# A fused attention and mixture-of-experts kernel: first chunk ahead of the loop, rows of x earlier in it, the branch moved up, pools that wait by tile

## The chip, the core and the metric

One program on one core of a Trainium2 chip. The metric is the time of one execution on the device in microseconds (us); lower is better. Five engines run their own instruction streams in order: TensorE (PE; its weight loads are listed as PEld), VectorE (DVE), ScalarE (ACT), GpSimd (POOL) and SyncE (SP, which issues most DMA transfers). They wait for each other through semaphores.

## What is computed

Three parts follow each other: a gated linear attention over 4 x 8 heads of 768 steps, a layer of eight experts in which each takes at most 384 of 3072 tokens (tokens choose in the order of their logits), and a dense ELU layer.

```python
# attention, per batch and head; f = sigmoid(f_logit)
for t in range(S):
    state = f[t, :, None] * state + outer(k[t], v[t])
    y[t] = q[t] @ state
x = y as 3072 rows of 384
# experts
logits = x @ w_gate
for idx in argsort(-logits.flatten()):
    tok, e = idx // E, idx % E
    if assigned[tok] >= 0 or counts[e] >= cap: continue
    assigned[tok] = e; counts[e] += 1
out[assigned == e] = relu(x[assigned == e] @ w1[e]) @ w2[e]
# dense layer
h = out @ w_in
return where(h > 0, h, exp(min(h, 0)) - 1) @ w_out
```

## The kernel before

**Attention.** The 3072 rows are cut into NJ = 24 chunks of 128 (six for each batch). All heads of a chunk go together, in four pairs. The order of the work is written by hand: one pass `j` of a loop from -5 to 23 holds steps of several chunks, and each engine runs its own share in that order. For a chunk: `load` (f, v, k and q by SyncE), `decayE` and `decayL` (an exponential and a logarithm on ScalarE, of two chunks at once; for the first two chunks one at a time), `decays` (L473, TensorE sums the logarithms with a triangular mask), `prepW` and `prepP` (L477, L481, exponentials of the sums on ScalarE), `prepK` and `prepQ` (L486, L490, k and q times these on VectorE), `scores` (L502, TensorE), `masked` (L523, VectorE), `turn` and `turned` (L509, L516: the keys turned on TensorE, copied out on ScalarE), `state`, `carry`, `carried` (L535 to L543), `ystep` (L554, L560), `yout` (L565), `xrows` (L574: TensorE turns y into rows of x and the logits of the gate), `xout` (L578), `xstore`, `lout` (L584). In a pass TensorE runs state(j), scores(j+1), turn(j+1), ystep(j), xrows(j-1), decays(j+3). The last chunk of each six has no turn and no state.

**Weights of the dense layer** ride along: `Conv` loads a block of 512 columns of 64-bit numbers per pass, unpacks it on VectorE (`bits`, L287 to L294), rounds it on ScalarE (`hi`, L301) and takes the difference on GpSimd (`lo`, L308), since a product is made of a high and a low half of each operand.

**Counting.** `best` finds each token's best expert, `reach` (L607) compares its logit with a grid of 256 thresholds, `counted` (L614) sums over tokens on TensorE. From the sums L760 to L769 find the threshold `least` above which no expert is over its 384.

**Ids.** `slots` gives each token above the threshold its place: sums on TensorE, a scan and sums on VectorE, then one-hot rows `oh` (L828 on ScalarE, L834 on VectorE) whose products with `R0` give the first 256 ids of the first expert (`pm0`, L840, read at L843) and with `Rm` all ids (`pm`, L849, read at L850). `gather0` (L857) fetches the first 256 rows of x, `gatherL` (L864) the logits of tokens without a place. `during` runs `feed` in between: it loads weights of an expert (`raw`, L213, six buffers), rounds them on ScalarE (`pc_h`, L229) and takes the low half on VectorE (`pc_l`, L222). Then all engines load `fi`, which says whether a general routine has to do the attention and the choice again, and branch at L871 (with these inputs the routine is skipped).

**Experts.** `xtrans` (L1095) transposes gathered rows, `F1` (L1113) multiplies with a block of w1, `F2` (L1100 to L1102) with a block of w2; eight of each make an expert. `tick` puts the steps of the late choice (L899 to L973: tokens without a place, round by round) between them. The dense layer (L1215 and on) follows each expert.

`spin` issues matmuls on a scratch tile whose result nobody reads.

**Pools.** Tiles come from pools that open and close. A pool opened on bytes of closed pools makes its tiles wait for every user of those.

## Time and profile before

| | us |
|---|---|
| median of 3 runs | 833.48 |
| runs | 838.24, 830.11, 833.48 |
| profiled execution, device time | 838.72 |
| its span, first to last instruction | 837.0 |
| TensorE busy, share of the span | 800.5, 96% |
| VectorE busy | 478.9, 57% |
| ScalarE busy | 414.8, 50% |
| GpSimd busy | 109.0, 13% |
| mean granted TensorE clock | 0.978 |

How the views are read. A row of the timeline or of the chain that ended last begins with its start and its length in us; then engine, line, operation, what is written and read, the shape, and a count where several were merged (their length is then that of the stretch). In brackets stands how long the engine was idle before it, and what ended that. A row of a table by stretch gives the stretch, its length, the busy time of each engine with its instructions, the granted TensorE clock (1.00 is 2.4 GHz, 0.50 is 1.2 GHz), the share of the DMA engines and their GB/s. Instructions on TensorE overlap; a matmul's row includes its way through the array.

### The profile page before, as it was taken

Reading aid. Unit: us, or ns where it says so; the run is one execution under the profiler, and the core shown is the slowest. Engines: PE = TensorE matmul, PEld = TensorE weight load, DVE = VectorE, ACT = ScalarE, POOL = GpSimd, SP = SyncE. Lnnn points to the kernel's source line nnn. Section 1 sums busy time; section 2 is a strip of 40 time slices with the busy share of each in tenths; the row PEclk is TensorE's granted clock in tenths of the full one; section 3 lists DMA queues with packets and bytes.
Section 4 is the critical chain, followed back from the end, with each engine's and each line's share of the span. In section 5 each row is a group of like instructions: output and inputs, shape, how many; then the busy total and the mean of one; then the engine's idle time right before and its main releaser. Section 6 shows DMA issues by size and latency. Waiting matters only on the chain.

```text
span 837.0 us, 15862 instructions
## 1 busy us (share of the span) xinstructions
PE 800.5 (96%) x6123; PEld 755.1 (90%) x6123; DVE 478.9 (57%) x1199; ACT 414.8 (50%) x883; POOL 109.0 (13%) x157
## 2 busy tenths in 40 slices
PE   7899999858989999999999999999999999999996
PEld 6788887658889999999999989999999999999996
DVE  5998888736676755675564345533354335434432
ACT  6566665313554544454445445544445445543442
POOL 2222222220242000300100031000120020001001
PEclk9999999868999999999999998999999999999999
DMA  9998986322043300420041036200051023002000
GB/s 267 261 290 266 287 247 177 89 56 63 1 135 101 98 10 1 138 70 1 13 140 38 1 105 189 76 20 0 20 162 38 1 85 95 29 1 67 1 1 28
DMA packets 41668, 76.75 MB, mean 92 GB/s; under 512 B 8816, under 2 KB 30576, under 8 KB 41584
## 3 DMA queue, kind: packets, MB, share of 16 engines
q1 hardware_dynamic: 38384, 66.20, 26.5%
q0 software_dynamic: 3200, 9.46, 3.5%
q8 instruction: 49, 0.80, 0.4%
q14 instruction: 35, 0.29, 0.1%
HBM read 66.09 MB, written 9.55 MB: 90 GB/s over the span
## 4 chain that ended last, share of the span: by engine, by line
PE 64%; issue 9%; DVE 4%; ACT 1%; POOL 1%; POOLq 0%; DVEq 0%; ACTq 0%
PE ha L1215 20%; PE ha L1113 12%; PE yo L1100 10%; PE yo L1102 10%; PE yo L1101 10%; PE ha L1095 1%; DVE pc_l L222 1%; POOL out L1279 1%; DVE oh L938 1%; DVE elu L1219 0%; PE rt L948 0%; DVE oh L940 0%; ACT h_h L1117 0%; DVE oh L941 0%; PE rt L928 0%
## 5 line engine op out<-in xcount | busy, mean ns | idle before, releaser
L1219 DVE SCALAR_TENSOR_TENSOR elu<-elu,ha 128x384 f32<-128x384 f32 (+2 forms) x128 | 70.8, 554 | 157.2 <-ACT elu L1218 157.2
L1215 PE MATMUL ha<-yt_h,wi_h 128*128 128x384 f32 (+2 forms) x384 | 130.7, 340 | 0.3 <-DVE elu L1219 0.3
L1215 PE MATMUL ha<-yt_h,wi_l 128*128 128x384 f32 (+2 forms) x384 | 129.6, 338 | 0.0
L1100 PE MATMUL yo<-wo_h,g_h 128*128 128x384 f32 x381 | 129.4, 340 | 0.0
L1102 PE MATMUL yo<-wo_h,g_l 128*128 128x384 f32 x381 | 128.5, 337 | 0.0
L1101 PE MATMUL yo<-wo_l,g_h 128*128 128x384 f32 x381 | 128.1, 336 | 0.0
L1215 PE MATMUL ha<-yt_l,wi_h 128*128 128x384 f32 (+2 forms) x384 | 126.1, 335 | 0.0
L1217 ACT ACTIVATE elu<-ha 128x384 f32<-128x384 f32 (+2 forms) x128 | 62.8, 491 | 115.7 <-PE ha L1215 114.1
L1082 ACT ACTIVATE g_h<-elu 128x384 fp32r<-128x384 f32 (+2 forms) x127 | 66.4, 523 | 70.0 <-DVE elu L1219 69.8
L1083 DVE TENSOR_TENSOR g_l<-elu,g_h 128x384 fp32r<-128x384 f32 (+2 forms) x112 | 64.5, 576 | 48.9 <-ACT g_h L1082 47.5
L1117 ACT ACTIVATE h_h<-ha 128x384 fp32r<-128x384 f32 (+2 forms) x72 | 32.7, 455 | 114.7 <-PE ha L1113 104.0
L1118 DVE SCALAR_TENSOR_TENSOR h_l<-ha,h_h 128x384 fp32r<-128x384 f32 (+2 forms) x72 | 36.9, 512 | 83.2 <-ACT h_h L1117 80.0
L1279 POOL DMA_INDIRECT out<-ot,permL x22 | 22.7, 1031 | 432.3 <-ACT ot L1277 428.9
L1113 PE MATMUL ha<-xt_h,pc_l 128*128 128x384 f32 (+2 forms) x216 | 72.0, 334 | 4.0 <-DVE pc_l L222 4.0
L222 DVE TENSOR_TENSOR pc_l<-raw,pc_h 128x384 fp32r<-128x384 f32 x144 | 74.6, 555 | 0.6 <-ACT pc_h L229 0.5
L1215 PEld LDWEIGHTS ha<-yt_h,wi_l 128*128 128x128 f32 x384 | 72.1, 188 | 2.2
L1215 PEld LDWEIGHTS ha<-yt_h,wi_h 128*128 128x128 f32 x384 | 72.2, 188 | 2.0 <-DVE elu L1219 0.5
L1215 PEld LDWEIGHTS ha<-yt_l,wi_h 128*128 128x128 f32 x384 | 71.9, 188 | 1.5
L1113 PE MATMUL ha<-xt_h,pc_h 128*128 128x384 f32 (+2 forms) x216 | 71.9, 333 | 0.6 <-ACT xt_h L1082 0.6
L1100 PEld LDWEIGHTS yo<-wo_h,g_h 128*128 128x128 f32 x381 | 71.6, 188 | 0.9 <-ACT g_h L1082 0.3
L1101 PEld LDWEIGHTS yo<-wo_l,g_h 128*128 128x128 f32 x381 | 71.6, 188 | 0.6
L1102 PEld LDWEIGHTS yo<-wo_h,g_l 128*128 128x128 f32 x381 | 71.6, 188 | 0.3 <-DVE g_l L1083 0.3
(253 smaller groups left out, 1523.3 us busy)
## 6 DMA issues: line engine op xcount, KB each, us to landing
raw<-w SPq DMA_DIRECT2D x144, 192.0 KB, 2.4
ld_kq<-kq SPq DMA_DIRECT2D x24, 448.0 KB, 9.7
r<-win SPq DMA_DIRECT2D x12, 512.0 KB, 5.5
r<-wout SPq DMA_DIRECT2D x12, 512.0 KB, 4.6
vt<-vP SPq DMA_DIRECT2D x12, 384.0 KB, 7.5
x_d<-x SPq DMA_DIRECT2D x24, 192.0 KB, 2.6
ld_f<-fP SPq DMA_DIRECT2D x11, 384.0 KB, 6.3
ld_f<-fP SPq DMA_DIRECT2D x2, 192.0 KB, 3.8
```

The lines of the kernel that those rows point to most:

```text
L222: nc.vector.tensor_tensor(l, RAW.pop(i), h.bitcast(F32), op=OP.subtract)
L1082: nc.scalar.activation(hi, src, AF.Copy)
L1083: (eng or nc.vector).tensor_tensor(lo, src, hi.bitcast(F32), op=OP.subtract)
L1100: nc.tensor.matmul(o, wh, mh, start=start, stop=False)
L1101: nc.tensor.matmul(o, wh, ml, start=False, stop=False)
L1102: nc.tensor.matmul(o, wl, mh, start=False, stop=stop)
L1113: nc.tensor.matmul(p[:, :n], a[:, d * 128:(d + 1) * 128], b[:, d, :n], start=i == 0, stop=i == 8)
L1117: nc.scalar.activation(h[:, :n], p[:, :n], AF.Relu)
L1118: nc.vector.scalar_tensor_tensor(l[:, :n], p[:, :n], 0.0, h[:, :n].bitcast(F32), op0=OP.max, op1=OP.subtract)
L1215: nc.tensor.matmul(p, a[:, d * 2048 + f * 128:d * 2048 + (f + 1) * 128], b[:, d, :N], start=i == 0, stop=i == 8)
L1217: nc.scalar.activation(e, p, AF.Relu, scale=-1.0)
L1219: nc.vector.scalar_tensor_tensor(e, e, -1.0, p, op0=OP.add, op1=OP.max)
```

## The change

The first chunk is issued ahead of the loop, which now begins at pass 0. In a pass TensorE runs state(j), turn(j+1), xrows(j-1), scores(j+1), ystep(j), decays(j+3); `xout`, `xstore` and `lout` move up by one chunk, and `hi` of the dense weights follows `xout`. k and q have three tiles of their own, and the third load is issued ahead of the loads of the gate weights. Some memsets and copies at the start change places; `spin` reads one constant tile. The checks `okp` to `badp` come after the last `reach`. In `slots` six weight blocks are rounded in two groups of three, and five low halves are taken on GpSimd (`lows`): two ahead of `gather0`, three behind it. The branch follows these; `Rm`, the product for all ids and `gatherL` come behind it, the product between the two parts (six and three matmuls) of the first two `F1`. The pools behind the attention let each tile wait only for the users of its own bytes.

```diff
-SPIN = (9, 24, 3, 7, 12)
-WARM = 22
+SPIN = (9, 24, 3, 10, 8, 4, 12)
+WARM = 14
+WARM2 = 4
...
+    def lows(n, eng):
+        for _ in range(n):
+            i = nxt["lo"]
+            h, l = PC[order[i]]
+            eng.tensor_tensor(l, RAW.pop(i), h.bitcast(F32), op=OP.subtract)
+            nxt["lo"] += 1
...
-            KQ[j] = ld.tile([112, 2, 4, 128], F32, name="ld_kq", bufs=3)
-            nc.sync.dma_start(KQ[j].rearrange("p n r t -> p (n r t)"), kq[j])
...
+    KQs = [att.tile([112, 2, 4, 128], F32, name=f"kq{i}") for i in range(3)]
+    KQ = {j: KQs[j % 3] for j in range(NJ)}
...
     load(0, "v")
-    for t in VT:
-        nc.gpsimd.memset(t[:, 768:], 0.0)
+    load(2, "kq")
+    nc.vector.memset(onesB, 1.0)
+    usum = att.tile([128, NJ], F32, name="usum")
+    nc.vector.memset(usum, 0.0)
...
-    spin(ps.tile([128, 1024], F32, name="sc"), WARM)
+    pre = ps.tile([128, 1024], F32, name="sc")
+    spin(pre, WARM)
     one, two = slice(0, 1), slice(1, 2)
-    for j in range(-5, NJ):
-
-        if j >= 3:
-            xstore(j - 3)
...
+    decayE(0, one)
+    decayL(0, one)
+    decays(0)
+    spin(pre, WARM2)
+    prepW(0)
+    prepP(0)
+    decayE(0, two)
+    decayL(0, two)
+    prepK(0)
+    prepQ(0)
+    turn(0)
+    scores(0)
+    decays(1)
+    turned(0)
+    masked(0)
+    decayE(2)
+    prepW(1)
+    prepP(1)
+    decayL(2)
+    prepK(1)
+    prepQ(1)
+    state(0)
+    ystep(0)
+    decays(2)
+    load(4, "f")
+    load(6, "f")
+    conv.load()
+    yout(0)
+    for j in range(NJ):
+
+        if j >= 2:
+            xstore(j - 2)
...
+        prepW(j + 2)
+        prepP(j + 2)
+
+        if j:
+            state(j)
+        turn(j + 1)
+        if j >= 1:
+            xrows(j - 1)
+        scores(j + 1)
+        turned(j + 1)
+        if j >= 1:
+            xout(j - 1)
         if j >= 1:
             conv.hi()
-        if j >= 2:
-            xout(j - 2)
...
-        if j >= 0:
-            state(j)
-        if j + 1 >= 0:
-            scores(j + 1)
-            turn(j + 1)
-            turned(j + 1)
...
-        if j >= 1:
-            xrows(j - 1)
-        if j + 3 >= 0:
-            decays(j + 3)
+        decays(j + 3)
...
-    g0 = ctx.enter_context(tc.tile_pool(name="g0", bufs=1))
+    g0 = ctx.enter_context(tc.tile_pool(name="g0", bufs=1, reuse_waits="tile"))
...
+        if ahead:
+            feed(3, False)
         R0 = tiles(3 * EARLY[0], 2, G)
...
+        if ahead:
+            feed(GAP_FEED - 3, False)
...
         V.tensor_scalar(fi, f1, 0.0, None, op0=OP.is_lt)
+        if ahead:
+            lows(2, G)
...
         V.tensor_scalar(perm0, pm0, 1536.0, None, op0=OP.add)
         gather0()
-        Rm = tiles(0, 28, V)
-        during()
-        spin(wm, SPIN[4])
-        for k in range(NJ):
-            nc.tensor.matmul(pm, oh[:, k, :], Rm[:, k, :], start=k == 0, stop=k == NJ - 1)
-        V.tensor_scalar(permE, pm, 1536.0, None, op0=OP.add)
-        V.tensor_copy(permF, pm)
+        if ahead:
+            lows(GAP_LOW - 2, G)
...
-    slots(lambda: feed(GAP_LOW + 1))
-    feed(GAP_FEED - GAP_LOW - 1, False)
-    gatherL()
+    slots(True)
     rv = nc.values_load(fi[0:1, 0:1], min_val=0, max_val=1, skip_runtime_bounds_check_because="a comparison gives 0 or 1")
     with tc.If(rv > 0):
...
-        gatherL()
+    Rm = tiles(0, 28, nc.vector)
...
+    spin(fh.tile([128, 512], F32, name="ha", bufs=3), SPIN[3])
+    xtrans(0)
+    spin(fh.tile([128, 512], F32, name="ha", bufs=3), SPIN[4])
+    F1a(0, 0)
+    F1a(0, 1)
+    pm = mt["tt"].rearrange("p a e c -> p (a e c)")[:, :28]
+    for k in range(NJ):
+        nc.tensor.matmul(pm, mt["oh"][:, k, :], Rm[:, k, :], start=k == 0, stop=k == NJ - 1)
+    F1b(0, 0)
+    F1b(0, 1)
+    nc.vector.tensor_scalar(permE, pm, 1536.0, None, op0=OP.add)
+    nc.vector.tensor_copy(permF, pm)
+    gatherL()
```

## Rows read from the trace of the kernel before

**Rows 1.** Busy time by stretch: the 100 us from 500 on

```profile
500.00:600.00 100.00, 98.90 (x517) 92.48 (x518) 45.19 (x81) 49.87 (x98) 2.95 (x4) 0.97 0.22 66
```

**Rows 2.** Who waited for whom, 40 to 140 us: engine, line, releaser; sum, times, longest

```profile
DVE am L523 <- PE sc L502: 12.6, 17, 1.4
```

**Rows 3.** Timeline of TensorE's weight loads, one pass of the loop

```profile
104.40 0.85 PEld L554 LDWEIGHTS y<-am,vt 128*64 128x64 f32 x16
...
106.01 0.97 PEld L574 LDWEIGHTS lp<-IW,yt 112*128 112x128 f32 x8 [0.18 <-issue]
107.08 0.83 PEld L473 LDWEIGHTS L<-mask,u 128*48 128x48 f32 x16
107.89 0.60 PEld L535 LDWEIGHTS kv<-vt,kn 128*64 128x64 f32 x16
```

**Rows 4.** Timeline of the opening, ScalarE

```profile
5.80 0.52 ACT L459 ACTIVATE u<-ld_f 128x384 f32<-128x384 f32 x1 [3.69 <-DVE usum L440]
```

**Rows 5.** Timeline of VectorE, chunks 2 and 3

```profile
18.06 0.95 DVE L486 TENSOR_TENSOR kk<-ld_kq,W 112x512 f32<-112x512 f32 x1 [0.54 <-DMA ld_kq<-kq]
...
24.33 1.21 DVE L523 TENSOR_TENSOR am<-sc,mask 128x1024 f32<-128x1024 f32 x1
...
25.73 0.68 DVE L486 TENSOR_TENSOR kk<-ld_kq,W 112x512 f32<-112x512 f32 x1
```

**Rows 6.** DMA, 0 to 40 us: GB/s in each of 40 slices

```profile
GB/s 0 12 270 345 303 393 315 284 256 304 132 285 358 360 238 283 250 331 401 280 222 282 242 262 229 292 265 271 388 289 256 367 253 256 156 127 132 163 131 323
```

**Rows 7.** Busy time by stretch, cut where the granted clock changes

```profile
148.50:151.90 3.40, 3.40 (x35) 2.70 (x35) 3.07 (x16) 0.74 (x2) 1.59 (x1) 0.50 0.24 64
...
172.40:192.90 20.50, 16.02 (x69) 14.19 (x69) 6.84 (x26) 5.10 (x12) 1.96 (x3) 0.50 0.15 42
```

**Rows 8.** Timeline behind the loop: first ids, and TensorE behind the branch

```profile
165.91 0.16 DVE L843 TENSOR_SCALAR permA<-pm 128x2 int32<-128x2 f32 x1 [0.30 <-PE pm L840]
...
173.27 1.65 PE L628 MATMUL ha<-triU,onesB 128*128 128x256 bf16 x7 [4.73 <-PEq L871]
```

**Rows 9.** Timeline at the loop's end: VectorE's last compares, GpSimd's subtraction

```profile
151.28 0.28 DVE L607 TENSOR_SCALAR ge<-grid,top 128x256 bf16<-128x256 bf16 x1
...
154.87 1.56 DVE L607 TENSOR_SCALAR ge<-grid,top 128x256 bf16<-128x256 bf16 x2
...
155.09 1.26 POOL L308 TENSOR_TENSOR wo_l<-w,wo_h 128x512 fp32r<-128x512 f32 x1 [4.97 <-ACT wo_h L301]
```

**Rows 10.** Timeline of the ids: VectorE's builds, GpSimd's multiply

```profile
162.59 2.77 DVE L834 TENSOR_TENSOR oh<-iota,lo 128x768 f16<-128x768 f16 x3
...
162.81 0.87 POOL L820 TENSOR_TENSOR Rm<-Rm,idc 128x48 f16<-128x48 f16 x1 [1.02 <-DMA raw<-w]
```

**Rows 11.** Chain that ended last, from the transposes to the second F1

```profile
174.92 1.33 PE ha L1095 x6
...
176.82 4.22 PE ha L1113 x18
...
181.48 0.42 DVE h_l L1118
```

**Rows 12.** Groups, 160 to 176 us: busy, mean ns | idle before, releaser

```profile
L864 POOL DMA_INDIRECT LU<-lg_d,permA x4 | 3.8, 953 | 1.2 <-issue 1.2
L857 POOL DMA_INDIRECT xg<-x_d,permA x2 | 2.8, 1410 | 3.0 <-DVE permA L843 2.7 <-issue 0.3
...
L849 PE MATMUL tt<-Rm,oh 128*128 128x28 f16 x24 | 0.8, 175 | 0.6 <-DVE Rm L820 0.6
```

**Rows 13.** Timeline of the first expert: a low half, the choice, a low half

```profile
186.76 0.58 PE L1102 MATMUL yo<-h_h,pc_l 128*128 128x256 f32 x1 [2.04 <-DVE pc_l L222]
...
191.34 0.18 DVE L917 TENSOR_TENSOR w<-LU,pen 128x32 f32<-128x32 f32 x1
...
193.39 0.39 PE L1113 MATMUL ha<-xt_h,pc_l 128*128 128x256 f32 x1 [0.50 <-DVE pc_l L222]
```

**Rows 14.** The page's DMA issues: weights of an expert

```profile
raw<-w SPq DMA_DIRECT2D x144, 192.0 KB, 2.4
```

More of the change, by code (lines that the diff above doesn't have):

```diff
@@ L372 @@
                             pattern=[[1, 128]], channel_multiplier=-1)
+    nc.gpsimd.memset(idn, 0.0)
+    nc.gpsimd.affine_select(out=idn, in_=idn, compare_op=OP.not_equal, fill=1.0, base=0,
+                            pattern=[[-1, 128]], channel_multiplier=1)
+    for t in VT:
+        nc.gpsimd.memset(t[:, 768:], 0.0)
     side = lambda pr, s: s if pr < 2 else 1 - s
@@ L875, with gather @@
         slots()
-        gatherL()
+    Rm = tiles(0, 28, nc.vector)
+    XG, XT, H, Y = {0: xg0}, {}, {}, {}
+    def gather(si):
+        if si >= len(subs) or si in XG:
+            return
+        need(si)
+        XG[si] = []
+        for t in range(len(subs[si][1])):
+            g = sb.tile([128, 384], F32, name="xg", bufs=3)
+            nc.gpsimd.indirect_dma_start(out=g, out_offset=None, in_=x_d,
+                                         in_offset=bass.IndirectOffsetOnAxis(ap=PERM[si][:, t:t + 1], axis=0))
+            XG[si].append(g)
@@ new lines, in F2 @@
+    def F2(si, f):
+        g = 8 * si + f
+        wh, wl = ready(g, 1)
+        used[1] = g - 1
+        h, l, n = H.pop(g)
+        if n == 128:
+            if f == 0:
+                Y[si] = fp.tile([128, 384], F32, name="yo", bufs=4)
+            mm3(Y[si], h[:, :n], l[:, :n], wh, wl, f == 0, f == 7)
+            return
+        if f == 0:
+            Y[si] = [fp.tile([128, 384], F32, name="yo", bufs=4) for _ in range(3)]
+        for d in range(3):
+            w = slice(d * 128, d * 128 + 128)
+            mm3(Y[si][d][:, :n], wh[:, w], wl[:, w], h[:, :n], l[:, :n], f == 0, f == 7)
@@ L1137 @@
-    spin(fh.tile([128, 512], F32, name="ha", bufs=3), SPIN[3])
-    xtrans(0)
-    F1(0, 0)
-    F1(0, 1)
     late = []
```

276 lines of the change are left out of this document (125 added, 151 removed).

## The prediction

> **What bounds the kernel now.** I read the granted clock first, since it changes the price of every matmul, then the busy table by stretch, the timeline of the opening, the weight loads of one pass of the loop, and the stretch between the loop and the first expert.
>
> The kernel has three stages. From the second expert on TensorE sets the time: it is busy 98.9 of the 100 us from 500 on [rows 1]. None of that work is edited, so what is saved ahead of it arrives at the end whole. The mean clock of 0.97 in that stretch [rows 1] is some 6 us at half clock; the change touches nothing there either.
>
> The first 140 us are the chunk loop. Between 40 and 140 us VectorE waited for TensorE's scores 17 times, 12.6 us in all [rows 2], while TensorE's weight loads follow each other with gaps of about 0.1 us [rows 3]: TensorE sets the pace. In the opening it does not: ScalarE starts its first exponential at 5.80 us, released by a small memset on VectorE and not by its data [rows 4]; VectorE then waits for the k and q of chunk 2 until 18.06, and masks chunk 2 only at 24.33 [rows 5]. DMA delivers 200 to 400 GB/s in nearly every microsecond from 2 to 34 [rows 6].
>
> The middle, from 148 us into the first expert, is a chain of waits, at half clock (1.2 GHz) for 3.4 us from 148.5 and for 20.5 us from 172.4 [rows 7]. The second fall comes while TensorE stands 4.73 us at the branch, until 173.27 [rows 8].
>
> **The change part by part.** The profiled execution took 838.72 us (span 837.02, 1.70 around it), 5.2 more than the median of the three runs. The sum is made against 838.72.
>
> *Opening.* The memset that held ScalarE now precedes VectorE's other work, so the exponential starts when the first half of f (192 KB) is there, some 3.3 us by the delivered bytes [rows 6]: 2.5 us earlier for chunk 0. Chunk 1's decays now stand behind chunk 0's exponentials on ScalarE, so its scores gain less, about 1 us. The third load of k and q moves ahead of the gate weights and two f loads, so the wait before 18.06 goes. Chunk 2 still needs chunk 1's mask, its own k and q products and the unpacking of two weight blocks, in the same order on VectorE; I make its mask 1.2 us earlier than 24.33. Then follow k and q of chunk 3 (used at 25.73 [rows 5]); their load stands on SyncE behind an f load that now waits for a later exponential. The full DMA queue [rows 6] covers that; without the cover the load would come up to 2.5 us later. I take 1.4 us: below, nothing, where the full queue decides; above, the 2.5.
>
> *Order in the loop.* The same matmuls run in the order state, turn, rows of x, scores, y, decays. After a change of the stationary tile's shape the next load starts late: at 107.08, not 106.98, after the rows of x; between decays and state, of nearly one shape, there is no gap (107.89 against 107.91) [rows 3]. Turn and rows of x both load 112 rows by 128, so one gap of 0.09 us goes in the 18 passes that have both: 1.6 us; bounds 0 and 1.8. Queued behind the rows of x are now the scores, and VectorE waits for those; it had 0.7 us to spare per pass (12.6 over 17 [rows 2]).
>
> *End of the loop.* The rows of the last chunk but one no longer stand between the last y and its own rows: 1.07 us (106.01 to 107.08 [rows 3]). That stretch ran at half clock [rows 7]; TensorE now idles less ahead of it, and of the at most 1.7 us that the clock costs there I take back 0.5. So 1.6 us, bounds 0.3 and 2.7. Six small checks move behind VectorE's last compare, in place of one of two compares; those took 1.56 us while GpSimd subtracted for 1.26 [rows 9]. I take nothing: between a loss of 1.0 and a gain of 0.7.
>
> *Ids.* Five subtractions go from VectorE to GpSimd, two of them beside the three one-hot builds. GpSimd's multiply of 48 columns took 0.87 us beside those builds (2.77 for the three) [rows 10], while its subtraction of 512 columns took 1.26 [rows 9]; so the engines hinder each other. One of 384 columns would take 0.95 us alone, an estimate (1.26 x 384/512). If one gets in between two builds, the last build is late by it: 1.0 us lost; bounds 0 (the builds ran at 0.92 each beside the multiply) and 2.0 for both. The Trainium skill (SBUF — State Buffer, "SBUF: two separate sides") says that a VectorE operation with two SBUF inputs and a GpSimd operation that reads SBUF take one port pair in turn, each for its whole length. By that rule both subtractions can come first, and the time would be 1.0 us higher than by my value; the 0.87 us agree with it, and no row shows who goes first.
>
> *Branch.* It now follows the first 256 ids, ready at 165.91; TensorE worked on until 168.54 before it stood at the branch [rows 8]. Its 4.7 us stay, but they now overlap the gather of x. TensorE is back 5.2 us after the ids, at half clock again after that idle time. Before, the second F1 ended 15.1 us after the ids, at 181.04 [rows 11]. Now: the two gathers end at 3.6 (0.5 to start, 2.8 busy, 0.3 between [rows 12]), three subtractions on GpSimd at 6.5, ten warming matmuls at 7.6 (seven took 1.65 [rows 8]). Then 1.3 for the transposes [rows 11], up to 1.9 for eight more warmers, 4.2 for F1's 18 matmuls and 0.8 for the ids among them [rows 12]: 15.8 at half clock. At full clock it starts at 7.0 and takes half: 11.4. TensorE has hardly a gap from 5.2 on, so I take a value between, 13.0: 2.1 us gained; bounds -0.7 and 3.7.
>
> *First expert.* From the second F1 to the fifth's wait (193.39 [rows 13]) passed 12.4 us, 2.04 of them in one wait for a low half and 0.50 in the last [rows 13]. Five low halves now lie ready instead of two, so these go. What is late next: the four gathers of logits now come after the last ids, which VectorE reads only behind its part of the second F1 (181.48 and 0.42 [rows 11]), about 1.1 us after it. Four gathers take 5.0 us (3.8 busy, 1.2 between [rows 12]), and the last lands some 2.4 us after it starts (as loads do [rows 14]): 1.3 + 3.8 + 2.4 = 7.5 after F1. VectorE's choice needs them; from its start to the release of the low half behind it went 2.05 us (191.34 to 193.39 [rows 13]), and the third F2 now waits for that: 9.6 after the second F1, against 13.2 before (12.4 and seven matmuls of 0.12). Of the 3.6 I take off 0.7, because TensorE idles 3 us there and may fall to 1.2 GHz. 2.9 us; bounds 0 and 6. From there on nothing is edited. The waits by tile let the weight loads start sooner; no wait of TensorE here is for those first six, so that adds nothing.
>
> The sum: 1.4 + 1.6 + 1.6 + 0 - 1.0 + 2.1 + 2.9 = 8.6, so 830.1. The profiled execution lies 5.2 above the median, and its half clock after 500 us [rows 1] is not among the terms; I take off 1.6 of that, a choice: **828.5 us**.
>
> **The rivals.** *More gained:* the logits land before they are needed, or the clock is back before F1. Then 3.0 more and the 0.7 in the first expert, 1.1 at the branch and 1.1 in the opening: 5.9, so 822.6. For it: 20.5 us at half clock [rows 7] are a large stake. Against: the gathers are plainly behind F1.
>
> *Hardly anything:* DMA decides the opening (0), no gap goes (0), the clock stays low up to the second F1 (-0.7), both subtractions come first (-2.0). With 1.6 and 2.9 that leaves 1.8: 838.7 - 1.8 - 1.6 = 835.3. For it: the full queue [rows 6], and a branch that stalls as long as before.
>
> *Slower:* the turn now comes before the scores, so TensorE needs a chunk's k product earlier. After one chunk's scores it does y (104.40 to 106.01), decays and state (107.08 to 108.49): 3.0 us [rows 3]; VectorE does mask, sum and k product in 2.1 (24.33 to 26.41 [rows 5]). If VectorE is over 0.9 us later than that, TensorE waits in each of 18 passes. GpSimd can hold a VectorE operation by 1.0 us (1.56 for two compares that take 0.28 alone [rows 9]); at 1.7 us late, which takes two such holds a pass, the price is 0.8 x 18 = 14.4: 842.9. Against: GpSimd's subtraction still falls beside the mask, as ScalarE's rounding ahead of it follows the same matmuls.
>
> **How the numbers follow.** Forecast 0.50, more gained 0.22, hardly anything 0.20, slower 0.08. A measurement tells about 1% from no change: 825.1 and 841.8 around 833.48. Below lie the second case and 0.10 from the forecast's low side: 0.32; above, most of the last: 0.07; between, 0.61. The range 820 to 836 takes in the first three cases with most of their bounds.
>
> **What would show it.** Right: the first exponential near 3.3 us; the mask of chunk 2 near 23; no gap between turn and rows of x, and no wait before the turn; TensorE back from the branch about 5 us after the ids; no wait for low halves before the third F2, and VectorE waiting for the logits there. Wrong: waits for the k product throughout the loop, the mask of chunk 2 at 24.3 as now, or half clock from the branch into the first expert as long as before.

## The result, and the profile after

| | before | changed |
|---|---|---|
| median of 8 runs, us | 836.39 | 827.77 |
| lowest to highest | 830.11 to 843.74 | 825.35 to 833.29 |
| profiled execution, device time | 838.72 | 828.17 |
| its span | 837.0 | 826.3 |
| mean granted TensorE clock | 0.978 | 0.988 |

The changed kernel takes 0.9911 of the time of before (95% interval 0.9884 to 0.9937). That is 0.9% faster, which the prediction put into "within 1%" (0.61); the forecast was 828.5 us in a range of 820 to 836.

The two profiled executions are 10.69 us apart in span. Six landmarks, each the start of an instruction in both traces, say where they came from (us; a stretch reaches from the landmark before it):

| stretch up to | before | changed | gained |
|---|---|---|---|
| mask of chunk 3 (VectorE) | 29.95 | 28.67 | 1.28 |
| mask of chunk 22 | 109.05 | 108.21 | 0.84 |
| comparison of the sums (`over`) | 17.79 | 15.09 | 2.70 |
| first ids (`perm0`) | 9.12 | 9.50 | -0.38 |
| third F1 (the second one's end) | 14.92 | 11.39 | 3.53 |
| first dense product | 27.79 | 24.35 | 3.44 |
| the end | 628.40 | 629.12 | -0.72 |

In the changed kernel `prepK` is L495, the mask L532, `xrows` L583, the branch L905, `F1` L964, `F2` L943 to L945, the low halves L238 on GpSimd and L223 on VectorE, the count for the late tokens L1037.

Opening, timelines of ScalarE, VectorE and TensorE:

```profile
3.33 0.52 ACT L468 ACTIVATE u<-ld_f 128x384 f32<-128x384 f32 x1 [1.22 <-DMA ld_f<-fP]
...
12.51 0.58 PE L544 MATMUL kv<-vt,kn 128*64 128x48 f32 x15 [2.53 <-DMA vt<-vP]
...
16.58 1.22 DVE L532 TENSOR_TENSOR am<-sc,mask 128x1024 f32<-128x1024 f32 x1 [4.28 <-PE sc L511]
...
22.16 1.67 DVE L302 SCALAR_TENSOR_TENSOR w<-r,w 128x512 int32<-128x512 int32 x1
23.75 1.21 DVE L532 TENSOR_TENSOR am<-sc,mask 128x1024 f32<-128x1024 f32 x1
...
27.17 0.69 DVE L300 SCALAR_TENSOR_TENSOR w<-r,w 128x512 int32<-128x512 int32 x1
```

VectorE in the kernel before:

```profile
16.30 1.23 DVE L523 TENSOR_TENSOR am<-sc,mask 128x1024 f32<-128x1024 f32 x1 [1.34 <-PE sc L502]
...
27.65 1.65 DVE L292 SCALAR_TENSOR_TENSOR w<-r,w 128x512 int32<-128x512 int32 x1
```

The first exponential now waits for its data alone, 2.5 us earlier than in [rows 4], and chunk 0 is masked at 9.01 instead of 12.53. Then TensorE stands 2.53 us for the first v, and chunk 1 is masked at 16.58, 0.3 us later than before. VectorE unpacks weights until it masks chunk 2 at 23.75, 0.6 earlier than in [rows 5]; one unpacking step ahead of the mask of chunk 3 takes 0.69 us instead of 1.65.

TensorE's weight loads in one pass of the loop, to be laid beside [rows 3]:

```profile
98.83 0.59 PEld L544 LDWEIGHTS kv<-vt,kn 128*64 128x64 f32 x16
99.47 0.39 PEld L518 LDWEIGHTS kt<-idn,kk 112*128 112x128 f32 x4
99.82 0.97 PEld L583 LDWEIGHTS lp<-IW,yt 112*128 112x128 f32 x8
...
104.40 0.59 PEld L544 LDWEIGHTS kv<-vt,kn 128*64 128x64 f32 x16
```

From state to state a pass takes 5.57 us (98.83 to 104.40); before it took 5.76. The rows of x start 0.35 us behind the turn.

The loop's end, VectorE's last unpacking step and TensorE's last y, in the kernel before:

```profile
143.22 1.75 DVE L294 SCALAR_TENSOR_TENSOR w<-r,w 128x512 int32<-128x512 int32 x1
...
148.52 1.98 PE L554 MATMUL y<-am,vt 128*64 128x128 f32 x16
```

The unpacking step, the last y and the last rows of x in the changed kernel:

```profile
141.10 0.69 DVE L302 SCALAR_TENSOR_TENSOR w<-r,w 128x512 int32<-128x512 int32 x1
...
145.35 1.09 PE L563 MATMUL y<-am,vt 128*64 128x128 f32 x16
...
147.80 1.14 PE L583 MATMUL lp<-IW,yt 112*128 112x104 f32 x8 [0.78 <-ACT yt L574]
```

The last y runs at full clock now, and TensorE waits 0.78 us for ScalarE's copy of it where the rows of the chunk before stood.

The ids and the branch, timelines of GpSimd, VectorE and TensorE:

```profile
157.35 3.57 DVE L873 TENSOR_TENSOR oh<-iota,lo 128x768 f16<-128x768 f16 x3
158.40 3.38 POOL L238 TENSOR_TENSOR pc_l<-raw,pc_h 128x384 fp32r<-128x384 f32 x2
...
164.47 2.89 POOL L238 TENSOR_TENSOR pc_l<-raw,pc_h 128x384 fp32r<-128x384 f32 x3
165.31 2.29 PE L637 MATMUL ha<-onesB 128*128 128x256 bf16 x10 [3.88 <-PEq L905]
165.97 2.11 DVE L824 TENSOR_TENSOR Rm<-i,tb 128x672 f16<-128x672 f32 x1 [4.35 <-DVEq L905]
167.84 1.17 PE L938 MATMUL ha<-idn,xg 128*128 128x128 f32 x6 [0.24 <-remote]
```

The three one-hot builds take 3.57 us beside two subtractions, 2.77 before [rows 10]. TensorE is back from the branch 3.84 us after the first ids; before it was 7.4 [rows 8].

The first expert, timelines of GpSimd, VectorE and TensorE:

```profile
178.06 0.95 POOL L900 DMA_INDIRECT LU<-lg_d,permA  x1 [0.30 <-issue]
179.03 0.16 POOL L1037 IOTA s<- 128x4 f32 x1
179.23 0.23 DVE L1039 TENSOR_SCALAR act<-s,tot 128x4 f32<-128x4 f32 x1 [4.22 <-POOL s L1037]
...
180.74 0.58 PE L945 MATMUL yo<-h_h,pc_l 128*128 128x256 f32 x1 [3.88 <-DVE pc_l L223]
```

Here is the new wait. TensorE stands 3.88 us in the second F2 for a low half; VectorE had stood 4.22 us ahead of that half, for a count that GpSimd makes only behind the four gathers of logits.

Busy time by stretch, cut where the granted clock changes:

```profile
148.50:151.90 3.40, 3.40 (x26) 1.94 (x25) 3.06 (x16) 1.01 (x2) 1.32 (x1) 1.00 0.25 64
...
161.69:168.52 6.83, 2.97 (x14) 2.03 (x15) 2.51 (x2) 0.00 (x0) 5.16 (x6) 0.50 0.38 100
168.52:178.76 10.24, 8.13 (x83) 7.38 (x81) 2.90 (x9) 4.44 (x11) 3.58 (x4) 1.00 0.28 79
178.76:185.59 6.83, 4.85 (x22) 4.85 (x23) 5.41 (x22) 0.80 (x2) 0.42 (x2) 0.50 0.37 106
236.80:240.20 3.40, 3.40 (x16) 3.09 (x15) 3.14 (x10) 1.48 (x3) 1.71 (x3) 0.50 0.56 174
```

The loop's end is at full clock now (half before, [rows 7]). Where 20.5 us were at 1.2 GHz, two stretches of 6.8 are: one behind the branch, one behind the new wait. The first two F1 fall between them, at 2.4 GHz. At 236.8 the clock fell for 3.4 us in the changed kernel alone, at 500 for 6.8 us in the one of before alone [rows 1]. So the clock does not account for the -0.72 of the last stretch; near 490 us TensorE also waited 3.2 us in the changed kernel, 1.50 of it for gathered rows of x, against 2.1 at the same place in the one of before.

### The profile page after: what moved, and what is told of

It reads as the page before. It is cut to its first block, busy times and chain, and to the rows that moved or that the text cites. A ratio compares the mean times of both kernels' runs of the same rounds, so it can differ in the third digit from the quotient of the medians.

```text
span 826.3 us, 15888 instructions
## 1 busy us (share of the span) xinstructions
PE 790.1 (96%) x6134; PEld 748.0 (91%) x6134; DVE 473.3 (57%) x1194; ACT 417.3 (50%) x883; POOL 114.3 (14%) x162
## 4 chain that ended last, share of the span: by engine, by line
PE 64%; issue 9%; DVE 3%; POOL 1%; ACT 1%; DMA 1%; POOLq 0%; another core or an unknown queue 0%; DVEq 0%; ACTq 0%
PE ha L1273 20%; PE ha L964 11%; PE yo L943 10%; PE yo L945 10%; PE yo L944 10%; PE ha L938 1%; DMA raw<-w 1%; DVE oh L1069 1%; POOL out L1337 1%; DVE pc_l L223 0%; POOL LU L900 0%; DVE elu L1277 0%; PE ha L637 0%; PE rt L1079 0%; DVE oh L1071 0%
## 5 line engine op out<-in xcount | busy, mean ns | idle before, releaser
L943 PE MATMUL yo<-wo_h,g_h 128*128 128x384 f32 x381 | 129.9, 341 | 0.0
L945 PE MATMUL yo<-wo_h,g_l 128*128 128x384 f32 x381 | 128.9, 338 | 0.0
L943 PEld LDWEIGHTS yo<-wo_h,g_h 128*128 128x128 f32 x381 | 71.9, 189 | 0.9 <-ACT g_h L925 0.3
L945 PEld LDWEIGHTS yo<-wo_h,g_l 128*128 128x128 f32 x381 | 71.9, 189 | 0.3 <-DVE g_l L926 0.3
L223 DVE TENSOR_TENSOR pc_l<-raw,pc_h 128x384 fp32r<-128x384 f32 x139 | 71.5, 552 | 0.6 <-ACT pc_h L230 0.5
L230 ACT ACTIVATE pc_h<-raw 128x384 fp32r<-128x384 f32 x144 | 67.5, 518 | 8.4 <-DMA raw<-w 8.4
L964 PE MATMUL ha<-xt_h,pc_h 128*128 128x384 f32 (+2 forms) x216 | 70.0, 326 | 0.5 <-DVE xt_l L926 0.4
```

The costliest lines, as they stand in the source:

```text
L223: nc.vector.tensor_tensor(l, RAW.pop(i), h.bitcast(F32), op=OP.subtract)
L230: nc.scalar.activation(h, RAW[i], AF.Copy)
L943: nc.tensor.matmul(o, wh, mh, start=start, stop=False)
L945: nc.tensor.matmul(o, wl, mh, start=False, stop=stop)
L964: nc.tensor.matmul(p[:, :n], a[:, d * 128:(d + 1) * 128], b[:, d, :n], start=i == 0, stop=i == 8)
```

## The experiments

Ten kernels are the changed one with a part undone, moved or added, one builds on the run `ids_first`, and one joins three edits. Medians of neighbouring variants differ by less than their intervals, so they are compared by the landmarks of their traces. The stretch from the mask of chunk 3 to the comparison of the sums came out at 123.30 to 123.32 us in the changed kernel and the six others of the table below that leave it alone; the opening spreads more, 27.2 to 30.0 us (`ids_first` and `x_release`, the two slowest, had half clock for 3.4 us from 12.4 and 12.1), the last stretch by 3.5 us though nothing is edited there, and the clock differs behind the branch.

| stretch up to | changed | iota_first | ids_first | branch_back | lows_behind | x_release | ids_two_lows | best1 |
|---|---|---|---|---|---|---|---|---|
| mask of chunk 3 | 28.67 | 28.36 | 29.98 | 27.23 | 28.38 | 29.97 | 28.01 | 27.96 |
| comparison of the sums | 123.30 | 123.32 | 123.30 | 123.30 | 123.31 | 123.30 | 123.32 | 121.51 |
| first ids | 9.50 | 9.51 | 9.51 | 9.50 | 8.71 | 9.53 | 9.53 | 9.53 |
| third F1 | 11.39 | 11.47 | 12.30 | 17.46 | 15.04 | 11.80 | 12.03 | 10.16 |
| first dense product | 24.35 | 23.72 | 19.39 | 18.74 | 23.70 | 25.09 | 27.73 | 19.24 |
| the end | 629.12 | 630.42 | 629.14 | 629.82 | 628.69 | 631.86 | 632.17 | 628.98 |

**What is late in the second F2?**

```diff
+    s4 = cst.tile([128, NU], F32, name="s4")
+    nc.gpsimd.iota(s4, ...)
     gatherL()
...
-        s4 = sb.tile([128, NU], F32, name="s4")
-        nc.gpsimd.iota(s4, ...)
```

> The changed kernel with one edit: GpSimd counts the places of the late tokens (the iota that late_start reads) ahead of the four gathers of logits instead of behind them. In the profile of the changed kernel TensorE waits 3.88 us in the second F2, for a low half that VectorE makes behind a comparison with that count, and VectorE stood 4.22 us before the comparison. Theory: the count waited only for GpSimd's queue, so the second F2 no longer waits (under 0.6 us at 176.6). VectorE then comes to its choice about 4 us earlier, at some 177.5, and there waits for the last logits (landed 180.85); the low half of the third F2 stands behind it, so the wait comes back one F2 later, 3.5 to 4.5 us long, and the third F2 starts 1 to 2 us earlier than its 184.32: about 826 us. Rival, the mechanism of the prediction: the logits themselves were late in the second F2; then the wait stays where it is, 3.9 us, and the time too.

827.86 us, 0.9905 of before (0.9877 to 0.9933). Timelines of VectorE and TensorE:

```profile
180.77 0.19 DVE L1048 TENSOR_TENSOR w<-LU,pen 128x32 f32<-128x32 f32 x1 [3.48 <-DMA LU<-lg_d,permA]
...
182.83 0.58 PE L945 MATMUL yo<-h_h,pc_l 128*128 128x256 f32 x1 [4.02 <-DVE pc_l L223]
```

The second F2 runs through, so it was the count behind the gathers. The wait is back one F2 later, 4.02 us, now for the logits themselves; this is the wait that the prediction had named. Removing the first of the two waits gained 0.6 us up to the dense product.

**Can both be early?** The product for all ids and the gathers move ahead of the first F1, with the count.

```diff
     spin(fh.tile([128, 512], F32, name="ha", bufs=3), SPIN[4])
-    F1a(0, 0)
-    F1a(0, 1)
     pm = mt["tt"].rearrange("p a e c -> p (a e c)")[:, :28]
...
     gatherL()
+    F1a(0, 0)
+    F1a(0, 1)
+    F1b(0, 0)
+    F1b(0, 1)
```

> The changed kernel with the count ahead of the gathers, as in the run before, and the product for all ids (24 matmuls, 0.8 us) and the gathers of logits ahead of the first two F1 instead of between their parts. The last logits then land some 3.3 us earlier, at about 177.5. Theory, that GpSimd's queue behind the second F1 sets the wait and the wait brings the clock down to 1.2 GHz (178.76 to 185.59 in the changed kernel): the wait of 3.88 us goes and with it the half clock, about 2.3 us of longer matmuls, so the first dense product starts near 191 instead of 197.21, and the time is 5 to 6.5 us less, 821 to 823. Rival: half clock follows the idle time at the branch and not this wait, then 3 to 4 us less; or the product holds F1 up, for the table Rm is ready only at 168.98, then 2 us less at most.

824.39 us, 0.9866 (0.9814 to 0.9918). The wait is down to this, TensorE in the third F2:

```profile
182.28 0.38 PE L945 MATMUL yo<-h_h,pc_l 128*128 128x256 f32 x1 [1.23 <-DVE pc_l L223]
```

From the third F1 to the dense product it takes 19.39 us instead of 24.35. Of the 5.0 us won, 0.9 is lost ahead (12.30 against 11.39), where this execution had half clock for 10.24 us behind the branch instead of 6.83. The first dense product starts at 194.48, not near 191: the opening took 1.3 more here, and the theory had not counted the loss ahead. The wait and the half clock behind it together are shown to cost the changed kernel 4 to 5 us in these traces; the medians lie 3.4 us apart, with intervals that overlap.

**What is the earlier branch worth?** Undone, with the first two F1 whole again:

```diff
     slots(True)
+    ids_all()
     rv = nc.values_load(fi[0:1, 0:1], ...)
```

> The changed kernel with the branch back behind the table Rm, the product for all ids and the issue of the gathers of logits, as in the kernel before; the first two F1 then run unsplit. Theory: TensorE reaches the branch some 4 us later (it has to wait for Rm), is back some 4 us later than 165.31, and the second F1 ends 4 to 6 us later than 172.84; but the logits are fetched meanwhile, so the wait of 3.88 us in the second F2 goes. Net 1 to 3 us slower than the changed kernel, 829 to 831. Rival: the branch costs the same wherever it stands, since x lands only 4.4 us after the gathers are issued; then the second F1 is at most 2 us later, the wait goes, and the kernel is 2 to 4 us faster than the changed one.

827.75 us, 0.9907 (0.9875 to 0.9939): as good as the changed kernel. The table shows why. The second F1 ends 6.1 us later after the ids (17.46 against 11.39); but the logits are fetched meanwhile, and up to the dense product the kernel then needs 5.6 us less (18.74). Up to the second F1 the earlier branch was worth 6 us, a part of it by the clock (half for 13.65 us here, for 6.83 in the changed kernel), and the gathers that were put behind it took them back.

**What are the five low halves worth?** On `ids_first`, where the logits are not late, two instead of five:

```diff
-GAP_LOW = 5
+GAP_LOW = 2
```

> The kernel with the ids ahead of the first F1 (run ids_first), with two low halves ready ahead of the first expert instead of five; VectorE makes the other three when their products come, as in the kernel before. Theory: it is the low halves that lie ready that shorten the first expert; without them waits of about 1 and 2 us come back in the third F1 and the first F2, and from the end of the second F1 to the first dense product pass 22 to 24 us instead of 19.4. Rival: the wait for the logits, some 1.5 us in that kernel, takes the place of the others, and then under 1 us is lost.

831.70 us, 0.9949 (0.9915 to 0.9983). TensorE in the first expert:

```profile
174.48 0.39 PE L964 MATMUL ha<-xt_h,pc_l 128*128 128x256 f32 x1 [1.19 <-DVE pc_l L223]
177.89 0.58 PE L945 MATMUL yo<-h_h,pc_l 128*128 128x256 f32 x1 [2.08 <-DVE pc_l L223]
...
194.28 0.41 PE L964 MATMUL ha<-xt_h,pc_l 128*128 128x256 f32 x1 [1.72 <-DVE pc_l L223]
```

The two expected waits are there, and three more, of 1.54, 0.94 and (last row) 1.72 us: the feed of weights stays behind through the whole expert. The stretch takes 27.73 us, 8.3 more than in `ids_first` and as long as before (27.79). With the logits on time this is the largest single part of the change.

**The subtractions beside the one-hot builds:**

```diff
-        if ahead:
-            lows(2, G)
...
-            lows(GAP_LOW - 2, G)
+            lows(GAP_LOW, G)
```

> The changed kernel with all five GpSimd subtractions behind the gathers of x, none beside the one-hot builds. Theory of the prediction: the two subtractions delay VectorE's builds; without them the three builds take 2.77 us as before, not 3.57, the first 256 ids come 0.8 us earlier after the threshold (8.7 instead of 9.5 us after the comparison of the sums), and the second F1 ends 0.5 to 0.8 us earlier. Rival: the five subtractions end later (some 170 instead of 167.4) and run beside the VectorE's table Rm and the low halves of x, so that F1 waits and what was won is lost: second F1 at 172.8 or later.

828.96 us, 0.9914 (0.9887 to 0.9941). The ids come after 8.71 us instead of 9.50, as the theory had it, and the rival is right as well: the second F1 ends 15.04 us after them. Timelines of GpSimd, VectorE and TensorE:

```profile
163.38 4.79 POOL L238 TENSOR_TENSOR pc_l<-raw,pc_h 128x384 fp32r<-128x384 f32 x5
...
164.91 3.98 DVE L824 TENSOR_TENSOR Rm<-i,tb 128x672 f16<-128x672 f32 x1 [4.35 <-DVEq L903]
...
168.64 1.51 PE L936 MATMUL ha<-idn,xg 128*128 128x128 f32 x6 [2.09 <-remote]
```

The transposes of x wait 2.09 us for something that no engine's row names, though x had landed at 165.60. GpSimd ended its subtractions at 168.17, and its next instructions stand at its branch. One of them counts up a semaphore; the view of the branch's line, in the changed kernel and then in this one:

```profile
L905 POOLq INC_SWDGE_SEM  x1: 241/241/241, 167.6 to 167.6; - x1
```

```profile
L903 POOLq INC_SWDGE_SEM  x1: 241/241/241, 168.4 to 168.4; - x1
```

TensorE's wait for x ends while it runs, at 167.73 and 168.53.

**Who tells TensorE that x is there?** Three subtractions go to VectorE behind the branch, and fewer warming matmuls stand ahead of the transposes:

```diff
-SPIN = (9, 24, 3, 10, 8, 4, 12)
+SPIN = (9, 24, 3, 4, 8, 4, 12)
...
-            lows(GAP_LOW - 2, G)
...
     xtrans(0)
+    lows(GAP_LOW - 2, nc.vector)
```

> The changed kernel, with the three subtractions that GpSimd makes between the gathers of x and the branch given to VectorE behind the branch, and four warming matmuls instead of ten ahead of the transposes. In the traces so far the transposes of x start 0.2 to 0.4 us after GpSimd has come to its branch (167.36 and 167.73 in the changed kernel, 168.17 and 168.53 with all five subtractions there, 171.22 and 171.75 with the gathers of logits there too), though x landed at 166.66, 165.60 and 166.71. Theory: TensorE learns of the gathered rows only from GpSimd at its branch, so the subtractions ahead of it were on the path: the transposes now start 4.7 to 5.2 us after the first ids, at the second landing, instead of 6.3, and the second F1 ends 1 to 1.5 us earlier after the ids than the 11.4 of the changed kernel, if the clock falls and rises at like places. Rival: the rows themselves are late, or TensorE is only then through its warming matmuls; then the transposes stay at 6.0 or more after the ids.

829.33 us, 0.9926 (0.9896 to 0.9957). Timelines of TensorE and VectorE:

```profile
167.26 0.86 DVE L824 TENSOR_TENSOR Rm<-i,tb 128x672 f16<-128x672 f32 x1 [4.30 <-DVEq L903]
...
167.64 1.49 PE L936 MATMUL ha<-idn,xg 128*128 128x128 f32 x6
```

The transposes start 4.84 us after the first ids (162.80), not 6.37, where the two halves of x landed at 167.14 and 167.93. With `lows_behind` this shows that in the other kernels it was GpSimd at its branch that released them. It took both halves of the edit: in the changed kernel the ten warming matmuls reach to 167.60, and the release came at 167.73. The second F1 does not gain by it here (11.80 after the ids): eight warming matmuls at half clock now stand between, and the clock came back later than in the changed kernel (172.55 against 168.52). The first half of the theory is shown, the gain is not.

**The order in the loop:**

```diff
-        if j >= 1:
-            xrows(j - 1)
         scores(j + 1)
+        if j >= 1:
+            xrows(j - 1)
```

> The changed kernel with one edit in the loop: the rows of x come behind the scores instead of behind the turned keys (order state, turn, scores, rows, y, decays). A whole pass took 5.76 us before and 5.57 in the changed kernel, a gain of 0.19 where the prediction had 0.09. Theory: neighbours with stationary tiles of one shape save the gap of 0.09 between the turn and its follower and, since the rows of x start without it, another 0.1 inside the rows' own eight matmuls (111 instead of 123 ns apart); then a pass goes back to 5.76 and the 20 passes from the mask of chunk 3 to that of chunk 23 take 113.04 + about 16 times 0.19, so 116. The prediction's own term gives a pass of 5.66 and 114.5. Rival: the gain comes from elsewhere in the new order (turn ahead of the scores, the first chunk issued ahead); then the pass stays at 5.57.

837.96 us, one run. A pass of TensorE's weight loads:

```profile
102.10 0.60 PEld L544 LDWEIGHTS kv<-vt,kn 128*64 128x64 f32 x16
...
103.28 0.97 PEld L511 LDWEIGHTS sc<-qq,kk 48*128 48x128 f32 x16
...
107.85 0.60 PEld L544 LDWEIGHTS kv<-vt,kn 128*64 128x64 f32 x16
109.17 0.52 PEld L511 LDWEIGHTS sc<-qq,kk 48*128 48x128 f32 x7 [0.72 <-PE kv L544]
```

The pass is back at 5.75 (102.10 to 107.85): the 0.19 hang on turn and rows of x being neighbours. That the equal shape of their tiles is the reason fits the rows, but no run shows it apart. From the mask of chunk 3 to that of chunk 23 it took 119.08 us, 3 more than the theory's 116: in passes without a turn the scores now wait (0.72 in the last row), so the rows of x also cover VectorE's products there, and two passes between 35 and 48 us were 0.9 and 1.0 longer, whose cause is open. The loop's end lost 3.1 us (18.23 from the mask of chunk 22 to the comparison of the sums), with half clock for 3.4 us from 146.84.

**The waits that the new order made:**

```diff
+        if j % 6 == 0:
+            carried(j)
         prepK(j + 2)
-        carried(j)
+        if j % 6:
+            carried(j)
```

> The changed kernel with one edit: for the first chunk of each six VectorE takes the state out of the sums (L552) ahead of the next product of k instead of behind it. In the changed kernel the passes that follow a batch's first chunk take 0.4 to 0.6 us longer than before (decays to decays 7.04, 6.69 and 7.30 us against 6.67, 6.18 and 6.70), with TensorE's state step 0.76 us behind its decays. Theory: the state step now comes first in a pass and waits for VectorE to free its accumulator; with the copy earlier the wait falls by 0.5 to 0.6 us in three passes, and the stretch from the mask of chunk 3 to that of chunk 23 takes 111.3 to 111.8 instead of 113.04. Rival: it waits for ScalarE's copy of the turned keys, or VectorE's mask is late too; then 112.8 or more.

824.99 us, one run. TensorE's state step of chunk 19 in the changed kernel and then in this one:

```profile
121.45 0.64 PE L544 MATMUL kv<-vt,kn 128*64 128x48 f32 x16 [0.48 <-DVE S L552]
```

```profile
120.49 0.64 PE L544 MATMUL kv<-vt,kn 128*64 128x48 f32 x16
```

The wait is gone, and each of the four passes concerned (decays to decays) is 0.60 us shorter. From the mask of chunk 3 to that of chunk 23 it still took 112.73, not 111.3 to 111.8: a pass at 62 to 69 us was 1.5 longer, and in it a load of k and q landed at 68.28, 3.4 later than its counterpart. `best1`, which holds the same edit, took 111.25; so the edit is worth about 1.8 us, and that long pass was this execution's own. The first of the four passes gains nothing: the one behind it is 0.6 longer, here and in `best1`.

**The opening, twice.** First the memset put back:

```diff
-    usum = att.tile([128, NJ], F32, name="usum")
-    nc.vector.memset(usum, 0.0)
...
     pend = att.tile([112, NJ, 4], F32, name="pend")
+    usum = att.tile([128, NJ], F32, name="usum")
+    nc.vector.memset(usum, 0.0)
```

> The changed kernel with the small memset that held the first exponential put back behind VectorE's other work at the start. ScalarE's first exponential then comes near 5.2 to 5.8 us instead of 3.33, and the mask of chunk 0 some 2 us later than 9.01. Theory of the prediction: of this gain about 1.2 us reaches chunks 2 and 3, so the mask of chunk 3 comes at 29.5 to 30.5 (28.67 in the changed kernel, 27.2 to 30.0 over its variants). Theory from the runs so far: the state step of chunk 0, ahead of the scores of chunk 1 on TensorE, waits for the first v, which lands at 10.9 to 12.4 us; so chunk 1 is masked 4.2 to 5.8 us behind that landing whatever the first exponential does, unless it is later than v, and the mask of chunk 3, 12.09 us behind that of chunk 1, moves by under 0.5 us for the memset.

830.20 us, one run. The first exponential is at 5.18, the mask of chunk 0 at 12.12 and that of chunk 3 at 30.78, 2.1 later than in the changed kernel: the theory that the first v alone sets it is wrong. TensorE's timeline shows the second cause:

```profile
10.00 2.08 PE L511 MATMUL sc<-qq,kk 48*128 48x128 f32 x16
```

The scores took 2.08 us instead of 1.16: TensorE had idled 2.26 us for the late exponential, and from 7.36 to 14.19 the granted clock was half.

Then an order that looked better: chunk 1's scores ahead of the state step that waits for v, k and q of chunk 3 loaded earlier, and the mask of chunk 2 ahead of the unpacking.

```diff
+    decays(2)
+    turn(1)
+    scores(1)
     state(0)
     ystep(0)
-    decays(2)
     load(4, "f")
+    load(3, "kq")
...
+        if j == 1:
+            masked(j + 1)
+            carry(j)
         if j >= 1:
             conv.bits(0)
```

> The changed kernel with the opening reordered: decays of chunk 2 and turn and scores of chunk 1 stand ahead of the first state step, which waits for the first v; the load of k and q of chunk 3 goes out ahead of the sixth f and of the two blocks of dense weights; and VectorE masks chunk 2 ahead of the unpacking of two weight blocks. In the traces so far the first v lands at 12.38 in the changed kernel, the mask of chunk 1 comes at 16.58 and moves from run to run between 15.1 and 17.9, and from there to the masks of chunks 2 and 3 it is 7.17 and 12.09 us in every one of them. Theory: the order of issue sets the opening, v ahead of the scores of chunk 1 and unpacking and the late k and q (landed 23.59) ahead of chunk 3. The mask of chunk 1 then comes near 13.6, that of chunk 2 near 19, that of chunk 3 at 24.5 to 26.5 instead of 28.7: 2 to 4 us less. Rival, that of the prediction: the DMA queues, full until about 34 us, set it; what one load gains the next loses, and chunk 3 is masked at 28 or later, or chunks 4 to 8 give the gain back.

834.29 us, 0.9989 (0.9960 to 1.0018): most of the change's gain lost. VectorE's timeline:

```profile
22.35 1.23 DVE L532 TENSOR_TENSOR am<-sc,mask 128x1024 f32<-128x1024 f32 x1 [2.68 <-PE sc L511]
...
28.39 0.68 DVE L495 TENSOR_TENSOR kk<-kq,W 112x512 f32<-112x512 f32 x1
...
33.18 1.23 DVE L532 TENSOR_TENSOR am<-sc,mask 128x1024 f32<-128x1024 f32 x1 [1.46 <-PE sc L511]
```

TensorE's scores of chunk 3:

```profile
31.05 2.08 PE L511 MATMUL sc<-qq,kk 48*128 48x128 f32 x16
```

Chunk 2 is masked 1.4 us earlier, and the unpacking then stands ahead of the product of chunk 3's k, at 28.39; its mask comes 4.5 us later than in the changed kernel. TensorE stood 3.84 us for that product, and the granted clock was half from 30.05 to 36.87: the scores took 2.08 us, and the next mask came 7.31 us after this one instead of 5.58. Chunk 1 did not gain either (masked at 16.98, not near 13.6), since the decays now ahead of its scores waited 1.98 us for ScalarE. So neither theory holds as put: the work was moved to a worse place on VectorE, and the clock fell behind the gap that this made on TensorE.

**The pools:** all `reuse_waits="tile"` taken out.

> The changed kernel with its pools waiting for all users of the closed pools' bytes, as in the kernel before. The prediction counted the finer waits at nothing. Theory: the weights of the first expert then are loaded only when the last user of the closed pools is done, at about 153.3 instead of 150.7, land near 156, and ScalarE's first three roundings end at about 157.6 instead of 155.9, just behind the 157.35 at which the one-hot rows can begin: the first ids come 0 to 0.5 us later after the comparison of the sums than the 9.50 us of the changed kernel, and nothing else moves. Rival: since rounding now stands ahead of the one-hot rows on ScalarE and two subtractions beside them on GpSimd, late weights hold up the ids by 1 to 3 us; then the finer waits are a condition of the new order.

826.74 us, one run. ScalarE's rounding starts at 155.04 instead of 153.61 and the first ids come 9.73 us after the comparison instead of 9.50; the later stretches are as in the changed kernel within 0.3 us (11.54 and 24.45). The finer waits are worth 0.2 us here, by one profile each.

**Three edits together:** `ids_first`, `carry_first`, and `x_release` with no warming matmuls behind the transposes.

> Three of the edits together on the changed kernel: the product for all ids and the gathers of logits ahead of the first F1 with the count ahead of them (ids_first), three subtractions on VectorE behind the branch with four warming matmuls ahead of the transposes and none behind them (x_release), and the state of a batch's first chunk taken out earlier (carry_first). If the gains add: 113.04 becomes 110.6 for the loop from chunk 3 to 23, the transposes start 4.9 us after the first ids and the second F1 ends 10.5 to 11.5 us after them, and from there to the first dense product 19 us instead of 24.35. Time 819 to 822.5. Rival: the edits compete, VectorE being late with table, low halves of x and three subtractions in one stretch; then the second F1 waits and the time is that of ids_first, 823 to 825.

819.69 us, 0.9819 of before (0.9776 to 0.9863). TensorE behind the branch, and its last long wait in the first expert:

```profile
165.41 0.84 PE L1002 MATMUL tt<-Rm,oh 128*128 128x28 f16 x24
...
176.21 0.39 PE L946 MATMUL yo<-h_h,pc_l 128*128 128x256 f32 x1 [1.08 <-DVE pc_l L223]
```

The product for all ids now fills the time in which ScalarE copies x out, and the second F1 ends 10.16 us after the ids although it ran partly at half clock. The gains add: 1.8 us in the loop, 1.2 up to the third F1, 5.1 in the first expert. It beats both kernels.

## Why the prediction was right, and where only its sum was

*The bound.* From the first dense product on the two kernels differ by 0.7 us in 629, the wrong way and less than the variants differ there (626.8 to 632.2 us). So what was saved ahead arrived.

*Opening: 1.4 foreseen, 1.28 measured, and that is luck.* The step that failed is that chunk 1's scores gain about 1 us: chunk 1 gained nothing (16.58 against 16.30; 15.1 to 17.9 over the variants), since its scores stand on TensorE behind a state step that waits for the first v. The gain was made behind it. From the mask of chunk 1 to that of chunk 3 the kernel before took 13.65 us, the changed one and eight variants 12.09: chunk 2's k product no longer waits for its load, and the unpacking step ahead of the mask of chunk 3 is 0.96 shorter. `memset_back` shows that in the new order the late exponential costs 2.1 us, a part of it by the clock; so the memset pays for what the order ahead of chunk 1 would lose. One profile is a weak measure here: the variants' own openings spread by 2.8 us. The mask of chunk 2 came at 23.75, not 23; the unpacking of weights, which the text only lists among what chunk 2 still needs, filled VectorE up to the mask.

*Order in the loop: 1.6 foreseen, 0.84 measured.* The place of the rows of x does what the text says, its size was off both ways. Per full pass 0.19 us went instead of 0.09, because the rows of x also run faster there (1.05 us long instead of 1.14). But with the state step first in a pass, the pass after each batch's first chunk waits 0.4 to 0.6 us for VectorE. The text looked at the new early need for k's product and not at that of the accumulator.

*Loop's end: 1.6 foreseen, 2.70 measured, by other parts.* 1.06 of it came ahead of the mask of chunk 23, which the text did not look at: VectorE's last unpacking step took 0.69 us instead of 1.75. Of the 1.64 behind that mask the clock gave 1.3, where I had taken back 0.5: the last y took 1.7 us instead of 3.0. The rows that no longer stand between gave 0.4 and not 1.07, because TensorE now waits 0.78 us for ScalarE's copy. That the moved checks cost nothing came out: from the last rows of x to the comparison both kernels take 4.2 us.

*Ids: 1.0 lost foreseen, 0.38 measured.* The builds lost 0.80, which `lows_behind` gives back; the sums ahead of them were 0.42 faster. Nearly half of that is VectorE's wait for TensorE's sums (0.87 us instead of 1.06), which ran at half clock before; the text's list of such stretches left that one out (158.7 to 162.1).

*Branch: 13.0 us up to the end of the second F1 foreseen, 11.39 measured.* That this is the end worked out for full clock (11.4) is luck: the parts named there, halved, give 11.1, and the clock was half until 7.05 us after the ids. TensorE was back after 3.84 us, not 5.2: it came to stand at the branch just as the ids came, and stood 3.88 us instead of 4.73. GpSimd's three subtractions stood in my sum ahead of the transposes; `lows_behind` and `x_release` show that they really hold them, by the release at GpSimd's branch.

*First expert: 2.9 foreseen, 3.44 measured, by other steps.* I had the third F2 start 10.3 us after the second F1 (9.6, and 0.7 for the clock); it was 11.46 (184.32). The step that failed is "VectorE's choice needs them": ahead of the choice VectorE needs the count, and that stood on GpSimd behind the gathers, so the wait came one F2 earlier. And "from there on nothing is edited" was wrong in effect: waits of 0.82 and 1.72 us for low halves later in the expert, outside the rows that I read, went with the feed that starts earlier. The third F2 came 1.2 us later than foreseen and the rest was 1.7 shorter; that these nearly cancelled is luck. Without the late logits the low halves give 8.3 us.

*The rivals.* "More gained" named the clock, back before F1, and the logits; the first half came true. Its sum took 1.1 for the branch where the text's own bounds (13.0 and 11.4) give 1.6. Of "hardly anything", both subtractions coming first (2.0) and a branch that stalls as long as before did not happen. The k product kept nobody waiting beyond 0.4 us in 100, so the slower case never began.

*The sum.* The terms were to give 8.6 us and gave 11.4, of which the last stretch took 0.7 back; single terms were off by 0.1 to 1.4. The device times of the profiled executions lie 10.55 apart; I had taken 1.6 off because that of before stood above the median. Over eight runs the medians lie 8.6 apart, that of before at 836.39 and not at 833.48. So the direction and most of the places were right, and that the total lies within 1 us of the forecast is luck in part.

## What to carry to other kernels

When a step is moved behind another on a queue, list what else stands behind it there: the gathers behind the moved branch, and a small count behind the gathers, cost nearly as much as the branch had won. Moving the count alone gained 0.6 us, since the logits were as late; count and gathers together gained 4 to 5. Two edits that each look like a gain can share one wait, so undo them one at a time and compare stretches of the trace; the medians of the changed kernel and of the one with its branch moved back agreed to 0.02 us while their stretches differed by 6. Where an engine is full, as VectorE in the opening from 17.7 us on, a step moved ahead delays the one behind it; in the one order tried this lost more than it won.

## What the runs showed of the hardware

Gathered rows were released to TensorE at GpSimd's branch, not by their landing: TensorE's wait for x ended 0.4 to 0.5 us after GpSimd's last work ahead of it (167.36 and 167.73 in the changed kernel, 168.17 and 168.53 in `lows_behind`, 171.22 and 171.75 in `branch_back`), and 0.1 to 0.3 us after GpSimd's INC_SWDGE_SEM at the branch began (167.6, 168.4, 171.5). The rows had landed at 166.66, 165.60 and 166.71. In `x_release`, where GpSimd is through with this by 164.5, the landing decided.

VectorE's compare that builds Rm took 0.86 us alone, 2.11 beside three subtractions of GpSimd and 3.98 beside five, and ended 0.72 us after the last of them both times (167.36 and 168.08, 168.17 and 168.89). So GpSimd kept it out through several instructions in a row. The Trainium skill (SBUF — State Buffer, "SBUF: two separate sides") says that whichever starts first has the shared ports for the whole of its instruction; the 3.98 us are more than one instruction of GpSimd (4.79 us for five), so here the turn did not change between them. Beside the two subtractions at the one-hot rows it did: there three builds lost 0.80 us in all, less than one subtraction.

TensorE stood 3.9 to 4.7 us at its conditional branch in every kernel. Most of it is one instruction, which takes ScalarE and GpSimd 0.05 us; the view of the branch's line in the changed kernel:

```profile
L905 PEldq COMPARE_BRANCH  x1: 3342/3342/3342, 161.8 to 161.8; - x1
```

The Trainium skill (Runtime: NRT & Kernel Launch, "Instruction fetch mechanics") says that a taken branch to code that is not yet loaded stalls for its fetch; the rows show the stall, not its cause.

The granted clock was half for 6.8 to 13.7 us around this branch in the changed kernel and its variants. It fell 0.26 us after TensorE came to stand there in the changed kernel, but between 1.4 us before that (`best1`) and 0.9 after it (`iota_first`) in the others, and 3.9 after it in the kernel before. So standing at the branch is not what sets it alone.
